# Attention and two MLPs in one kernel: loads issued in another order, and one addition of the weights' decoding moved from VectorE to GpSimd

## The chip, the cores and the metric

The kernel runs on one core of a Trainium2 chip. The metric is the device time of one execution in microseconds (us). TensorE multiplies matrices, VectorE and ScalarE work on elements, GpSimd does small element work and issues some of the transfers, and SP's queue issues most of the others.

## The reference

Three stages follow one another on 2 x 3008 rows of 256 columns. All is float32.

```python
scores = (1.0 / S) * z @ z.T                 # per batch, z is 3008 x 64
x = u * (np.maximum(scores, 0.0) ** 2 @ v)   # attention without a softmax
h = x @ moe_w_in                             # 6016 x 256 @ 256 x 2048
P = a[0] + a[1]*h + a[2]*h**2 + a[3]*h**3
Q = 1.0 + abs(b[0])*abs(h) + abs(b[1])*h**2
x = (P / (Q + 1e-06)) @ moe_w_out            # 2048 x 256
h = x @ moe2_w_in
out = (np.maximum(h, 0) + alpha * np.minimum(h, 0)) @ moe2_w_out
```

The four weight matrices arrive as 64-bit floats, each as a low and a high 32-bit word.

## The kernel before

Every float32 operand of TensorE is split into a high part that the fast format holds and the rest, a low part; a product is the sum of three matmuls. For z the two parts are stacked in one tile (zA), with a swapped copy (zB).

Attention (stream A) takes 12 blocks of 512 query columns (6 for each batch). A block has 12 steps, kp = 0 to 11, of 256 key rows each: `a_scores` makes the scores, ScalarE and VectorE make relu, square and the parts ahi and alo, and `a_values`, three steps behind (LAG_A), multiplies them with the parts of v (vt). At the end of a block `a_end` multiplies with u (the tile ut, loaded by `a_u`) and stores the result in DRAM (xd). The first MLP (m1) works on 12 blocks of 512 rows, each in 8 steps of 256 hidden columns, and stores to DRAM (x2d); the second MLP (m2) does the same and stores the output.

The main program emits steps. For the first 36 it emits stream A alone; then it weaves 40 steps of m1 into the rest of stream A; then the rest of m1 with m2. Beside that it decodes weights: `load_w` (16 tiles of m1's weights, in the first 36 steps and shortly after) and `spill_w` (16 tiles of m2's, every fifth step but not in steps 64 to 75, where batch 1's v is loaded). `decode` is a chain of six VectorE instructions and one ScalarE instruction on 128x512 words (L148 to L158); the last adds the part from the low word. The raw words come through GpSimd's queue into two buffers (tag "wr").

A scheduler orders each engine's instructions by its own idea of time and by a priority, which is the place in the program (`tc.high_priority(EARLY)` moves some forward). The order on each engine and queue is fixed when the kernel runs: an instruction that waits holds all behind it. A tile waits until a buffer of its tag is free. The raw v of batch 1, the raw z of batch 1, ut, x and the results share two buffers (tag "raw", RAW = 2); for batch 0, raw z and v have many early buffers (tag "big").

Of the kernel before, what the change touches and what calls it, by code (L numbers as in the profile page):

```python
# [7 lines left out]
F32 = mybir.dt.float32  # L8
# [4 lines left out]
ALU = mybir.AluOpType  # L13
# [28 lines left out]
def relu2_attention_rational_mlp_prelu_mlp(  # L42
# [47 lines left out]
    def raw_tile(nm, early=False):  # L90

        if early:
            return big.tile([P, 1024], F32, tag="big", name=nm)
        return tmp.tile([P, 1024], F32, tag="raw", name=nm, bufs=RAW)
# [16 lines left out]
    def load_rows(t, src, r0, n):  # L111

        full, rest = divmod(n, P)
        if full:
            nc.sync.dma_start(
                out=t[:, 0:full, :],
                in_=src[r0 : r0 + full * P, :].rearrange("(c p) d -> p c d", p=P),
            )
        if rest:
            for p0 in (0, HALF):  # L120
                nc.sync.dma_start(
                    out=t[p0 : p0 + rest, full, :], in_=src[r0 + full * P : r0 + n, :]
                )

    vt = {}

    def load_v(b, kp):

        raw = raw_tile("vraw", b == 0)
        r3 = raw.rearrange("p (c d) -> p c d", c=4)  # L130
        r0 = kp * 2 * P
        load_rows(r3, v[b], r0, min(S - r0, 4 * P))
        for i in range(2):
            t = big.tile([P, 2, 2, D], F32R, tag="big", name="vt")
            split(t[:, 0], t[:, 1], r3[:, 2 * i : 2 * i + 2, :], on_act=b > 0 or (kp > 0 and i == 0))
            if kp + i == NKP - 1:

                h2 = t[HALF:P, 0, 1].bitcast(F32)
                nc.vector.tensor_tensor(t[HALF:P, 1, 1], h2, h2, ALU.subtract)
            vt[b, kp + i] = t  # L140

    def decode(raw):

        low, high = raw[:, :, 0], raw[:, :, 1]
        w = tmp.tile([P, 2, 512], F32R, tag="t", name="dec", bufs=TT)
        val, ulp = w[:, 0].bitcast(F32), w[:, 1].bitcast(F32)

        nc.vector.tensor_scalar(val, high.bitcast(F32), BOUND, -BOUND, ALU.min, ALU.max)  # L148
        nc.scalar.activation(val, val, AF.Copy, scale=2.0**-112)
        vali = val.bitcast(I32)  # L150
        nc.vector.tensor_scalar(
            vali, vali, 3, 2**31 - 1, ALU.logical_shift_left, ALU.bitwise_and
        )
        nc.vector.scalar_tensor_tensor(vali, high, -(2**31), vali, ALU.bitwise_and, ALU.bitwise_or)

        nc.vector.tensor_scalar(ulp.bitcast(I32), vali, -(2**23), None, ALU.bitwise_and)
        nc.vector.scalar_tensor_tensor(ulp, low.bitcast(U32), 2.0**-52, ulp, ALU.mult, ALU.mult)
        nc.vector.tensor_tensor(val, val, ulp, ALU.add)  # L158
        return w

    def words(src):
# [71 lines left out]
    def load_z(b, g):  # L233

        raw = raw_tile("zraw", b == 0)
        n = qn[g]
        nc.sync.dma_start(out=raw[:, 0:n], in_=zt[b, :, g * QB : g * QB + n])
        if n % P:
            nc.sync.dma_start(out=raw[:, n : n + HALF], in_=zt[b, :, S - HALF : S])
            n += HALF  # L240
        t = zp.tile([P, QB], F32R, tag="z", name="zA")
        with tc.high_priority(EARLY):
            nc.vector.tensor_copy(t[:, 0:n], raw[:, 0:n])
            nc.vector.tensor_tensor(
                t[HALF:P, 0:n], raw[HALF:P, 0:n], t[HALF:P, 0:n].bitcast(F32), ALU.subtract
            )
        if (b, g) == (0, 0):
            zB[b, g] = zp.tile([P, QB], F32R, tag="z", name="zB")
            nc.scalar.copy(zB[b, g][HALF:P, 0:n], raw[HALF:P, 0:n])
            nc.vector.tensor_tensor(  # L250
                zB[b, g][0:HALF, 0:n], raw[0:HALF, 0:n], t[0:HALF, 0:n].bitcast(F32), ALU.subtract
            )
        zA[b, g] = t
# [16 lines left out]
    def a_begin(b, j):  # L270

        if (b, j) in zB:
            return
        n = qn[j]
        t = zp.tile([P, QB], F32R, tag="z", name="zB")
        for p0 in (0, HALF):
            nc.sync.dma_start(
                out=t[p0 : p0 + HALF, :n].bitcast(F32),
                in_=zA[b, j][HALF - p0 : P - p0, :n].bitcast(F32),
            )  # L280
        zB[b, j] = t
# [110 lines left out]
    def a_u(b, j):  # L392
        n = qn[j]
        t = tmp.tile([P, ND, QB], F32, tag="raw", name="ut", bufs=RAW)
        nc.sync.dma_start(
            out=t[:, :, :n],
            in_=ut_in[b, :, j * QB : j * QB + n].rearrange("(e p) s -> p e s", p=P),
        )
        uts[b, j] = t
# [7 lines left out]
        nc.sync.dma_start(out=xd[b, j][:, :, :n], in_=t[:, :, :n])  # L407


    def load_x(src, n, pool):  # L410
        raw = tmp.tile([P, ND, QB], F32, tag="raw", name="xr", bufs=RAW)
        nc.sync.dma_start(out=raw[:, :, :n], in_=src[:, :, :n])
        return split_x(raw, n, pool)

    def split_x(src, n, pool):
        hs, ls = [], []
        for d in range(ND):
            hi = pool.tile([P, QB], F32R, tag="x", name="xhi")
            lo = pool.tile([P, QB], F32R, tag="x", name="xlo")
            split(hi[:, :n], lo[:, :n], src[:, d, :n])  # L420
            hs.append(hi)
            ls.append(lo)
        return hs, ls
# [83 lines left out]
    g2 = {}  # L507
    acc2 = {}

    def m2_begin(q):  # L510
        if q != LAST:
            x2[q] = load_x(x2d[q], bn[q], late["x"])

    def m2_hidden(q, jp):
        n = bn[q]
# [15 lines left out]
    def m2_last(q, jp):  # L531

        n, r0 = bn[q], q * QB
        if jp == 0:
            acc2[q] = [
                psa.tile([P, ND, QB], F32, tag=f"acc{e}", name="acce")[:, 0] for e in range(ND)
            ]
        hi, lo = g2.pop((q, jp))
        for e in range(ND):
            acc = acc2[q][e][:, :n]  # L540
            half(acc, e, w2ot[jp], hi, lo, n, jp == 0, jp == NJ - 1)
            if jp < NJ - 1:
                continue

            parts = [(0, n)] if e == 0 else [(0, n // 2), (n // 2, n)]
            for i, (c0, c1) in enumerate(parts):
                t = tmp.tile([P, 2 * QB], F32, tag="t", name="oe", bufs=TT)
                copy, queue = ((nc.scalar.copy, nc.sync), (nc.vector.tensor_copy, nc.scalar))[i]
                copy(t[:, 0 : c1 - c0], acc[:, c0:c1])
                queue.dma_start(  # L550
                    out=out[e * P : (e + 1) * P, r0 + c0 : r0 + c1], in_=t[:, 0 : c1 - c0]
                )

    def m2_back(q, jp):
        if q == LAST:
# [21 lines left out]
    def a_stream():  # L577

        pend = []

        def drain(upto):
            while len(pend) > upto:
                q, kp = pend.pop(0)
                a_values(*q, kp)
                if kp == NKP - 2:
                    a_u(*q)
                if kp == NKP - 1:
                    a_end(*q)

        for q in blocks:  # L590
            b, j = q
            if q == (0, 0):
                load_z(0, 0)
                load_z(0, 1)
                load_v(0, 0)
            a_begin(b, j)
            for kp in range(NKP):
                if q == (0, 0) and kp % 2 == 0:
                    if kp + 4 < NKP:
                        load_z(0, kp // 2 + 2)  # L600
                    if kp + 2 < NKP:
                        load_v(0, kp + 2)
                a_scores(b, j, kp)
                pend.append((q, kp))
                drain(LAG_A)
                if j == NQ - 1 and b + 1 < B:
                    if kp % 2 == 1:
                        load_z(b + 1, kp // 2)
                    if (kp - LAG_A) % 2 == 1 and kp > LAG_A:
                        load_v(b + 1, kp - LAG_A - 1)  # L610
                if j == 0 and b > 0:
                    k0 = kp + NKP - LAG_A - 1
                    if k0 < NKP and k0 % 2 == 0:
                        load_v(b, k0)
                yield
        drain(0)
        yield
# [21 lines left out]

    ga = a_stream()  # L640
    g1s = m_stream(m1_hidden, m1_back, m1_begin, m1_end, range(NB), LAG_M, x1)
    g2s = m_stream(m2_hidden, m2_back, m2_begin, m2_end, range(NB), LAG_M)
    w1 = [w for jp in range(NJ) for w in ((w1i, w1it, jp, True), (w1o, w1ot, jp, False))]
    w2 = [w for jp in range(NJ) for w in ((w2i, w2it, jp, True), (w2o, w2ot, jp, False))]
    fills = list(w2)
# [18 lines left out]
    for st in range(HEAD, na):  # L664
# [11 lines left out]
        if st >= na - 1 - NKP + LAG_A and fills:  # L676
            for _ in range(2):
                if len(fills) > 4 - (BIG - 28):
                    f = fills.pop(0)
                    fill_w(f[1], f[2])  # L680

    zctx.close()
    assert len(fills) <= BIG - 2 * NJ - NKP + 4
    late["x"] = ctx.enter_context(tc.tile_pool(name="xp2", bufs=XP))
    late["w"] = ctx.enter_context(tc.tile_pool(name="late", bufs=max(len(fills), 1)))
    for f in fills:
        fill_w(f[1], f[2])

    left = (NB - 1) * NJ - KEEP
    steps = NB * NJ - n1  # L690
    for st in range(steps):
# [45 lines left out]
```

## Time and profile before

| | us |
|---|---|
| median of 3 runs | 1559.61 |
| lowest and highest | 1559.13 and 1562.73 |
| the profiled execution | 1560.04 |
| its span, first to last instruction | 1558.3 |

The granted TensorE clock was 1.00 over the span. In the page an engine's line gives its busy time, its share of the span and its number of instructions. In the order of time a row gives start, duration, engine, line, operation and tiles, and in brackets how long the engine had been idle and what ended that. "SPq" is SP's queue.

### The profile page before, as it was taken

The numbers are of one execution on the slowest core, as the hardware profiler recorded it, in microseconds if no ns is written. First come the engines' busy times: TensorE is split into PE (matmuls) and PEld (weight loads), VectorE is DVE, ScalarE is ACT, GpSimd is POOL, SyncE is SP. The second block draws the span as 40 slices with busy tenths as digits, with TensorE's granted clock in tenths as the row PEclk, the third lists the DMA queues.
The fourth block names the chain that finished last, engine by engine and source line by source line (L and its number), as shares of the span: only waits on it lengthen the run. The fifth ranks groups of instructions, "written<-read, shape, count | busy, mean of one in ns | idle before, by whom it ended". The sixth has DMA issues, their size and how long they took to land.

```text
span 1558.3 us, 18042 instructions
## 1 busy us (share of the span) xinstructions
PE 1547.0 (99%) x6896; PEld 1284.4 (82%) x6896; DVE 1397.4 (90%) x1495; ACT 1194.3 (77%) x1465; POOL 53.9 (3%) x93
## 2 busy tenths in 40 slices
PE   9999999999999999999999999999999999999998
PEld 7888888888887888888788888888888888888888
DVE  8999999999899999898999989999899999898864
ACT  8999998998999989897667666666666666666654
POOL 1010000000000000001000000000000000000000
PEclk9999999999999999999999999999999999999999
DMA  6342111331212212135101000000101010001000
GB/s 190 115 129 87 54 55 41 115 119 34 82 34 68 74 55 68 53 95 178 38 1 41 26 29 14 28 27 28 41 0 41 1 41 28 24 0 42 14 1 24
DMA packets 37910, 83.16 MB, mean 53 GB/s; under 512 B 5168, under 2 KB 15040, under 8 KB 37824
## 3 DMA queue, kind: packets, MB, share of 16 engines
q1 hardware_dynamic: 26128, 48.34, 9.6%
q0 software_dynamic: 11552, 33.57, 6.9%
q8 instruction: 54, 0.88, 0.2%
q14 instruction: 32, 0.26, 0.1%
q10 hardware_dynamic: 144, 0.10, 0.0%
HBM read 52.70 MB, written 26.48 MB: 51 GB/s over the span
## 4 chain that ended last, share of the span: by engine, by line
PE 84%; DVE 6%; issue 4%; DMA 2%; ACT 2%; POOL 0%; SPq 0%; POOLq 0%; DVEq 0%; ACTq 0%
PE acc L363 20%; PE acca L363 11%; PE h L343 10%; PE h L344 10%; PE h L345 10%; PE acc L372 10%; PE acca L372 5%; PE s L322 3%; PE s L323 3%; DMA zraw<-in_z_dram 1%; PE acce L353 1%; DVE alo L109 1%; DVE ghi L484 0%; ACT r L328 0%; DMA wraw<-in_moe_w_out_dram 0%
## 5 line engine op out<-in xcount | busy, mean ns | idle before, releaser
L363 PE MATMUL acc<-ghi,w 128*128 128x512 f32 (+1 forms) x1472 | 366.5, 387 | 0.0
L363 PEld LDWEIGHTS acc<-ghi,w 128*128 128x128 f32 x1472 | 275.3, 188 | 54.7 <-ACT ghi L106 0.3
L343 PE MATMUL h<-xhi,w 128*128 128x512 f32 (+1 forms) x768 | 295.4, 386 | 1.2 <-DVE t L477 0.8
L344 PE MATMUL h<-xlo,w 128*128 128x512 f32 (+1 forms) x768 | 295.9, 386 | 0.0
L345 PE MATMUL h<-xhi,w 128*128 128x512 f32 (+1 forms) x768 | 295.8, 385 | 0.0
L363 PE MATMUL acca<-ahi,vt 128*128 128x512 f32 (+1 forms) x1152 | 289.4, 386 | 2.4 <-ACT ahi L106 1.9
L363 PEld LDWEIGHTS acca<-ahi,vt 128*128 128x128 f32 x1152 | 215.5, 188 | 46.1 <-ACT ahi L106 4.0
L522 ACT ACTIVATE m<-h,sal 128x512 f32<-128x512 f32 (+1 forms) x192 | 127.3, 680 | 111.4 <-PE h L345 109.9
L470 ACT ACTIVATE sq<-h 128x1024 f32<-128x1024 f32 (+1 forms) x96 | 96.9, 1010 | 139.7 <-PE h L345 130.1
L372 PE MATMUL acc<-glo,w 128*128 128x512 f32 (+1 forms) x736 | 195.9, 387 | 0.3 <-DVE glo L487 0.3
L109 DVE TENSOR_TENSOR alo<-r,ahi 128x1024 fp32r<-128x1024 f32 (+2 forms) x133 | 158.2, 1190 | 30.3 <-ACT ahi L106 11.0
L343 PEld LDWEIGHTS h<-xhi,w 128*128 128x128 f32 x768 | 144.1, 188 | 31.7 <-ACT sq L480 1.2
L344 PEld LDWEIGHTS h<-xlo,w 128*128 128x128 f32 x768 | 144.2, 188 | 28.7 <-DVE xlo L109 1.1
L345 PEld LDWEIGHTS h<-xhi,w 128*128 128x128 f32 x768 | 144.2, 188 | 27.5
L109 DVE TENSOR_TENSOR glo<-m,ghi 128x1024 fp32r<-128x1024 f32 (+1 forms) x96 | 115.1, 1199 | 55.5 <-PE acc L363 42.3
L372 PEld LDWEIGHTS acc<-glo,w 128*128 128x128 f32 x736 | 137.7, 188 | 28.2 <-DVE glo L487 0.8
L523 DVE SCALAR_TENSOR_TENSOR m<-h,sg,m 128x512 f32<-128x512 f32 (+1 forms) x192 | 138.1, 735 | 16.7 <-ACT m L522 15.3
L328 ACT ACTIVATE r<-r 128x1024 f32<-128x1024 f32 (+1 forms) x143 | 150.0, 1051 | 2.0
L372 PE MATMUL acca<-alo,vt 128*128 128x512 f32 (+1 forms) x552 | 149.3, 386 | 0.2 <-DVE alo L109 0.2
L325 ACT ACTIVATE r<-s 128x512 f32<-128x512 f32 (+1 forms) x244 | 135.3, 589 | 17.3 <-DVE t L486 13.8
L106 ACT CAST ahi<-r 128x1024 fp32r<-128x1024 f32 (+2 forms) x133 | 135.9, 1024 | 1.3 <-PE acc L372 0.8
L474 DVE SCALAR_TENSOR_TENSOR ab<-sq,cb,ab 128x1024 f32<-128x1024 f32 (+1 forms) x96 | 120.7, 1257 | 11.4 <-ACT ab L471 11.3
(92 smaller groups left out, 2135.3 us busy)
## 6 DMA issues: line engine op xcount, KB each, us to landing
wraw<-in_moe_w_in_dram POOLq DMA_DIRECT2D x16, 512.0 KB, 4.2
wraw<-in_moe_w_out_dram POOLq DMA_DIRECT2D x16, 512.0 KB, 3.9
wd<-dec POOLq DMA_DIRECT2D x32, 256.0 KB, 2.3
w<-wd POOLq DMA_DIRECT2D x16, 512.0 KB, 3.9
x2d<-x SPq DMA_DIRECT2D x11, 512.0 KB, 2.6
xr<-x2d SPq DMA_DIRECT2D x11, 512.0 KB, 3.3
out_dram<-ot SPq DMA_DIRECT2D x11, 512.0 KB, 2.9
vraw<-in_v_dram SPq DMA_DIRECT2D x10, 512.0 KB, 5.6
```

The lines of the kernel that those rows point to most:

```text
L106: nc.scalar.copy(dst_hi, src)
L109: nc.vector.tensor_tensor(dst_lo, src, dst_hi.bitcast(F32), ALU.subtract)
L325: nc.scalar.activation(r[:, i, :n], s, AF.Relu, scale=1.0 / S)
L328: nc.scalar.activation(r[:, :, :n], r[:, :, :n], AF.Square)
L343: nc.tensor.matmul(acc, w_hi, hi, start=first, stop=False)
L344: nc.tensor.matmul(acc, w_hi, lo, start=False, stop=False)
L345: nc.tensor.matmul(acc, w_lo, hi, start=False, stop=last)
L363: nc.tensor.matmul(acc[:, e, :n], w[:, k, i, e * P : (e + 1) * P], hi[i], start=first and i == 0 and k == 0, stop=False,)
L372: nc.tensor.matmul(acc[:, e, :n], w[:, 0, i, e * P : (e + 1) * P], lo[i], start=False, stop=last and i == both - 1,)
L474: nc.vector.scalar_tensor_tensor(ab, sq, b1, ab, ALU.mult, ALU.add)
L522: nc.scalar.activation(t[:, i], h, AF.Copy, scale=sal[:, f : f + 1])
L523: nc.vector.scalar_tensor_tensor(t[:, i], h, sg[:, f : f + 1], t[:, i], ALU.mult, ALU.max)
```

## The change

Six things change. (1) In the first block, groups 3 and 4 of z are loaded at step 2 and group 5 at step 4 (before: 3 at step 2, 4 at step 4, 5 at step 6). (2) The first two ut tiles get a one-column GpSimd copy that reads the last z tile, so their loads wait for it. (3) The loads of v and their splits are two functions; for batch 1 the raw words go into the two buffers of the weight words, and each load is issued one group of two steps before its split. (4) The addition at the end of `decode` runs on GpSimd. (5) `load_x` returns the raw tile; m2's first load is emitted before the attention's buffers are given up and its split before the last loop. (6) The last block's second half is copied by ScalarE and stored in one piece, as the first half is.

```diff
-        raw = raw_tile("vraw", b == 0)
+        if b == 0:
+            raw = raw_tile("vraw", True)
+        else:
+            raw = wr.tile([P, 1024], F32, tag="wr", name="vraw")
...
+        vraw[b, kp] = r3
+
+    def split_v(b, kp):
+        r3 = vraw.pop((b, kp))
...
-        nc.vector.tensor_tensor(val, val, ulp, ALU.add)
+        nc.gpsimd.tensor_tensor(val, val, ulp, ALU.add)
...
+        if b == 0 and j < RAW:
+
+            nc.gpsimd.tensor_copy(t[:, 0, 0:1], zA[0, NQ - 1][:, 0:1].bitcast(F32))
...
-        return split_x(raw, n, pool)
+        return raw
...
+    def m2_load(q):
+        x2r[q] = load_x(x2d[q], bn[q])
+
     def m2_begin(q):
-        if q != LAST:
-            x2[q] = load_x(x2d[q], bn[q], late["x"])
+        if q == LAST:
+            return
+        if q not in x2r:
+            m2_load(q)
+        x2[q] = split_x(x2r.pop(q), bn[q], late["x"])
...
-            parts = [(0, n)] if e == 0 else [(0, n // 2), (n // 2, n)]
-            for i, (c0, c1) in enumerate(parts):
-                t = tmp.tile([P, 2 * QB], F32, tag="t", name="oe", bufs=TT)
-                copy, queue = ((nc.scalar.copy, nc.sync), (nc.vector.tensor_copy, nc.scalar))[i]
...
+            nc.scalar.copy(t[:, 0:n], acc)
+            nc.sync.dma_start(out=out[e * P : (e + 1) * P, r0 : r0 + n], in_=t[:, 0:n])
...
-                    if kp + 4 < NKP:
-                        load_z(0, kp // 2 + 2)
+                    for g in {0: (2,), 2: (3, 4), 4: (5,)}.get(kp, ()):
+                        load_z(0, g)
...
-                    if (kp - LAG_A) % 2 == 1 and kp > LAG_A:
-                        load_v(b + 1, kp - LAG_A - 1)
-                if j == 0 and b > 0:
-                    k0 = kp + NKP - LAG_A - 1
-                    if k0 < NKP and k0 % 2 == 0:
-                        load_v(b, k0)
+
+                k0 = kp - LAG_A - 1 if j == NQ - 1 else kp + NKP - LAG_A - 1
+                b1 = b + (j == NQ - 1)
+                if (j == NQ - 1 or j == 0) and 0 < b1 < B and k0 % 2 == 0:
+                    if 0 <= k0 < NKP:
+                        split_v(b1, k0)
+                    if 0 <= k0 + 2 < NKP:
+                        load_v(b1, k0 + 2)
...
+    m2_load(0)
     zctx.close()
...
+    m2_begin(0)
```

## Rows read from the trace of the kernel before

**Rows 1.** The page, busy us and share of the span.
```profile
PE 1547.0 (99%) x6896; PEld 1284.4 (82%) x6896; DVE 1397.4 (90%) x1495; ACT 1194.3 (77%) x1465; POOL 53.9 (3%) x93
```

**Rows 2.** TensorE's waits, ten rows: us in total, times, longest.
```profile
PE acca L363 <- ACT ahi L106: 1.9, 3, 1.5
PE wps L101 <- DVE one L211: 1.4, 1, 1.4
PE sp L322 <- DVE zA L244: 0.9, 1, 0.9
PE h L343 <- DVE t L477: 0.8, 1, 0.8
...
PE acca L363 <- DVE ahi L337: 0.2, 1, 0.2
```

**Rows 3.** The chain that ended last, in order of time: start, us, what.
```profile
3.17 8.22 DMA zraw<-in_z_dram
...
158.38 1.81 PE acca L363 x8
```

**Rows 4.** Order of time, 0 to 14 us, SP's queue and TensorE.
```profile
2.10 1.02 SPq L395 DMA_DIRECT2D ut<-in_u_dram  x2
...
8.69 0.39 PE L323 MATMUL s<-zB,zA 128*128 128x512 f32 x1
...
13.31 0.47 PE L322 MATMUL sp<-zA 128*128 128x512 f32 x1
```

**Rows 5.** Order of time, 10 to 38 us, around the last z group.
```profile
10.89 0.43 SPq L239 DMA_DIRECT2D zraw<-in_z_dram  x1
...
36.28 0.69 DVE L244 TENSOR_TENSOR zA<-zraw,zA 64x512 fp32r<-64x512 f32 x1
...
37.12 0.47 PE L322 MATMUL sp<-zA 128*128 128x512 f32 x1 [0.88 <-DVE zA L244]
```

**Rows 6.** Order of time, 320 to 328 us, around a v load.
```profile
320.48 0.38 SPq L115 DMA_DIRECT2D vraw<-in_v_dram  x1
...
325.33 0.62 ACT L106 CAST vt<-vraw 128x512 fp32r<-128x512 f32 x1 [2.88 <-DMA vraw<-in_v_dram]
...
327.76 1.89 PE L363 MATMUL acca<-ahi,vt 128*128 128x448 f32 x8 [1.48 <-ACT ahi L106]
```

**Rows 7.** Order of time, SP's queue at 736 us.
```profile
736.78 0.54 SPq L412 DMA_DIRECT2D xr<-x2d  x1
```

**Rows 8.** Tile wraw: ns min/median/max; who waited for it (us, times).
```profile
L165 POOL COPY wraw<-zA x2: 653/948/1242, 17.2 to 18.4; 128x1 f32<-128x1 f32 x2
...
DVE dec L148: 2.8, 3
```

**Rows 9.** Tile dec: ns min/median/max, first and last start.
```profile
L158 DVE TENSOR_TENSOR dec<-dec x32: 679/684/693, 30.8 to 664.7; 128x512 f32<-128x512 f32 x32
...
L108 DVE CAST w<-dec x16: 406/422/487, 31.5 to 136.3; 128x512 fp32r<-128x512 f32 x16
```

**Rows 10.** Groups of GpSimd: busy us, mean ns, idle before.
```profile
L221 POOL TENSOR_TENSOR sal<-sc,sg 128x16 f32<-128x16 f32 x1 | 0.2, 215 | 0.0
...
L224 POOL TENSOR_TENSOR cb<-sc,cb 128x2 f32<-128x2 f32 x1 | 0.2, 187 | 0.0
```

**Rows 11.** Order of time, VectorE and TensorE, 17 to 61 us.
```profile
17.18 1.23 DVE L109 TENSOR_TENSOR alo<-r,ahi 128x1024 fp32r<-128x1024 f32 x1
...
57.97 1.22 DVE L109 TENSOR_TENSOR alo<-r,ahi 128x1024 fp32r<-128x1024 f32 x1
...
60.40 1.07 PE L372 MATMUL acca<-alo,vt 128*128 128x512 f32 x4
```

**Rows 12.** Busy us by stretch: PE, PEld, DVE, ACT, POOL, clock, DMA.
```profile
40.00:140.00 100.00, 100.00 (x443) 82.66 (x442) 95.16 (x156) 92.51 (x115) 10.84 (x15) 1.00 0.38 118
```

**Rows 13.** Tile oe, the last store: ns min/median/max.
```profile
L549 ACT COPY oe<-acce x2: 319/400/480, 1553.0 to 1554.1; 128x384 f32<-128x384 f32 x1, 128x192 f32<-128x192 f32 x1
...
L549 DVE COPY oe<-acce x1: 358/358/358, 1554.4 to 1554.4; 128x192 f32<-128x192 f32 x1
```

More of the change, by code (lines that the diff above doesn't have):

```diff
@@ L125, in relu2_attention_rational_mlp_prelu_mlp @@
     vt = {}
+    vraw = {}
     def load_v(b, kp):
-        raw = raw_tile("vraw", b == 0)
+        if b == 0:
+            raw = raw_tile("vraw", True)
+        else:
+            raw = wr.tile([P, 1024], F32, tag="wr", name="vraw")
         r3 = raw.rearrange("p (c d) -> p c d", c=4)
@@ L407, in a_end, with load_x @@
         nc.sync.dma_start(out=xd[b, j][:, :, :n], in_=t[:, :, :n])
-    def load_x(src, n, pool):
+    def load_x(src, n):
         raw = tmp.tile([P, ND, QB], F32, tag="raw", name="xr", bufs=RAW)
         nc.sync.dma_start(out=raw[:, :, :n], in_=src[:, :, :n])
-        return split_x(raw, n, pool)
+        return raw
     def split_x(src, n, pool):
@@ L508, in relu2_attention_rational_mlp_prelu_mlp @@
     acc2 = {}
+    x2r = {}
+    def m2_load(q):
+        x2r[q] = load_x(x2d[q], bn[q])
     def m2_begin(q):
-        if q != LAST:
-            x2[q] = load_x(x2d[q], bn[q], late["x"])
+        if q == LAST:
[3 more added lines that the diff above has]
+        x2[q] = split_x(x2r.pop(q), bn[q], late["x"])
     def m2_hidden(q, jp):
@@ L543, in m2_last @@
                 continue
-            parts = [(0, n)] if e == 0 else [(0, n // 2), (n // 2, n)]
-            for i, (c0, c1) in enumerate(parts):
-                t = tmp.tile([P, 2 * QB], F32, tag="t", name="oe", bufs=TT)
-                copy, queue = ((nc.scalar.copy, nc.sync), (nc.vector.tensor_copy, nc.scalar))[i]
[L549 to L552, printed above, removed]
+            t = tmp.tile([P, 2 * QB], F32, tag="t", name="oe", bufs=TT)
+            nc.scalar.copy(t[:, 0:n], acc)
+            nc.sync.dma_start(out=out[e * P : (e + 1) * P, r0 : r0 + n], in_=t[:, 0:n])
     def m2_back(q, jp):
@@ L595, in a_stream @@
                 load_v(0, 0)
+                split_v(0, 0)
             a_begin(b, j)
@@ L598, in a_stream @@
                 if q == (0, 0) and kp % 2 == 0:
-                    if kp + 4 < NKP:
-                        load_z(0, kp // 2 + 2)
+                    for g in {0: (2,), 2: (3, 4), 4: (5,)}.get(kp, ()):
+                        load_z(0, g)
                     if kp + 2 < NKP:
                         load_v(0, kp + 2)
+                        split_v(0, kp + 2)
                 a_scores(b, j, kp)
@@ L641, in relu2_attention_rational_mlp_prelu_mlp @@
     g1s = m_stream(m1_hidden, m1_back, m1_begin, m1_end, range(NB), LAG_M, x1)
-    g2s = m_stream(m2_hidden, m2_back, m2_begin, m2_end, range(NB), LAG_M)
+    g2s = m_stream(m2_hidden, m2_back, m2_begin, m2_end, range(NB), LAG_M, x2)
     w1 = [w for jp in range(NJ) for w in ((w1i, w1it, jp, True), (w1o, w1ot, jp, False))]
```

## The prediction

> **What bounds the kernel now.** I began with the page's busy times [rows 1]: TensorE is busy for 1547.0 us of a span of 1558.3, VectorE for 90% of it. So only what TensorE loses can be won back. The second view is the list of TensorE's own waits [rows 2]: ten rows, 6.6 us in all, of which 1.4 us lies before the first data and no single one is over 1.5 us. The third is the chain of work in order of time [rows 3], which gives the pace: eight full matmuls in 1.81 us, 0.227 us each. With it the order of time shows losses that the list of waits leaves out: the distance between two starts, less the matmuls between. Four places of some size lie where the edits touch.
>
> (a) The start. Between the starts at 8.69 and 13.31 us lie 13 matmuls, 13 x 0.227 = 2.95 us of 4.62, so 1.7 us are lost [rows 4]. The matmul at 13.31 needs the third group of z, whose transfer is on the chain from 3.17 on for 8.2 us [rows 3]. Ahead of it in SP's queue stand two ut loads at 2.10 [rows 4].
> (b) At 36 us. TensorE's start at 37.12 follows 0.9 us of waiting for VectorE's L244 on the last z group; with the restart about 1.0. The raw words of that group had been issued at 10.89, while L244 ran at 36.28 [rows 5]. So VectorE's order is late here, not the transfer.
> (c) At 327 us. A v load is issued only at 320.48; ScalarE stands still in its order for 2.9 us until it has landed, starts the cast at 325.33, and then makes ahi late for the values at 327.76: 1.5 us, about 1.6 with the restart [rows 6].
> (d) The passage from attention to the two MLPs: 0.8 us of waiting for L477 [rows 2], about 0.9 with the restart.
>
> These are 1.7 + 1.0 + 1.6 + 0.9 = 5.2 us. The rest of the list is 6.6 - 1.4 - 1.9 - 0.9 - 0.8 = 1.6 us in small pieces.
>
> **The change, part by part.**
>
> Start: each of the first two ut loads gets a GpSimd copy in front that waits for the last z group, so they leave the first 10 us. The third z group then has 1 MB less before it. The loss need not vanish, since the values matmuls in the same stretch wait for ScalarE [rows 2]. Bounds 0 and -1.7; I take half, -0.8. The two added copies stand in GpSimd's queue, with weight loads behind them; like the copies already there they cost 0.65 to 1.24 us each [rows 8]. A weight load that they make late is the same kind of delay as the one that the additions cause, and is priced with it.
>
> z order: groups 3 and 4 come with one step, the last at step 4 in place of 6. As its L243 and L244 now stand earlier in the program, I expect them earlier in VectorE's order. Bounds 0 and -1.0; I take -1.0, since L244 has to come only 1 us sooner and its raw words were asked for 25 us before.
>
> v loads of batch 1: they leave the two raw buffers, which they shared with z, ut, x and the results, for the two buffers of the weight words, and each is issued one group ahead of its split. During these steps no weights are spilled. A group is two attention steps with at least 32 matmuls (some 7 us), against 4.8 us from the issue at 320.48 to the cast [rows 6]. On SP's queue a v load that waits for its buffer would hold the z loads, the zB copies and the xd stores behind it; that can come only from the last spill before, or from a split that is late. Bounds 0 and -1.6; I take all, -1.6.
>
> m2's first load and split come earlier in the program. The load hardly can: it takes one of two raw buffers and goes out at 736.78, directly behind the last xd store [rows 7]. What can move is the order of the splits behind it, while the wait at L477 is the first MLP's own chain. Bounds 0 and -0.9; I take -0.2.
>
> Last store: two copies, ScalarE's 0.32 us and then VectorE's 0.36, become one of 384 columns, which took 0.48 for the other half [rows 13]: 0.2 us less, and a transfer of twice the size behind it. I take 0.
>
> The additions: 32 instructions of 0.684 us leave VectorE [rows 9], 22 us in all. TensorE gains nothing from that by itself, as it waits for VectorE only in the places above. What they cost on GpSimd is not in the trace. The nearest rows are its two-input instructions of 2 and 16 columns, 187 and 215 ns [rows 10]: 2 ns a column, so 0.19 + 512 x 0.002 = 1.2 us, an estimate from these two rows; VectorE's 0.684 is the lower bound. What matters more is whether VectorE can work beside it. The trace shows that GpSimd waits: a copy of a single column took up to 1.24 us [rows 8] while VectorE ran a subtraction of 1.23 us from 17.18 [rows 11]. The other direction isn't shown. The Trainium skill (SBUF — State Buffer, Who interferes with whom) says that a VectorE instruction with two SBUF inputs contends with a GpSimd instruction that reads SBUF, and that the one that comes second is blocked until the first has finished. By that rule each addition would stop VectorE for its own length; by VectorE's freed time alone there would be no loss.
>
> I work out both from rows. Of the 16 decodes before 140 us, 15 fall between 40 and 140 [rows 9], where VectorE is busy 95.2 of 100 us [rows 12]. If each addition holds VectorE for 1.2 us in place of its own 0.684, that is 15 x 0.52 = 7.8 us more: 103.0 us of work in 100. The 3.0 us too many meet a lead: an alo that ends at 59.19 is used at 60.40 [rows 11], 1.2 us ahead, the closest that I found in this stretch; most are near 3 us ahead. So it costs TensorE 0 to 3 us. In addition, the next weight load may now stand behind the addition on GpSimd's queue, 1.2 us late; three decodes wait for their load already, 2.8 us in all [rows 8], and there VectorE stops in its order, with alo behind. If that hits half of the 15, it is 7 x 1.2 = 8.4 us more, of which VectorE's 4.8 us of idle time can take some: up to 8 us in all for TensorE once the lead is used up. Without any exclusion the cost is 0. I take +1.0, nearer to the free end, since the lead and the idle time come first; bounds 0 and +8. The other 16 additions are spread up to 665 us [rows 9], one in 33 us, against VectorE's 10% of idle time: 0.
>
> Sum: -0.8 - 1.0 - 1.6 - 0.2 + 1.0 = -2.6 us. The profiled execution took 1560.04 us, its span 1558.3 and 1.7 around it, so it comes to 1557.4; the median of the runs shown is 1559.61, 0.4 lower, and gives **1557.0 us**.
>
> **Rivals.**
> *VectorE becomes the bound while the weights are decoded (slower).* The place is 40 to 140 us. It decides from the point where an addition costs VectorE more than its idle time and a lead of 3 us can carry: (4.8 + 3)/15 = 0.52 us above 0.684, so from 1.2 us of blocking on, exactly my estimate. For it: 95% busy, and the copies that were blocked. Against it: the lead, and that part of VectorE's work may run beside. With the late loads +8, and -2 from the moves: 1565.6. The Trainium skill's rule above speaks for it. Chance 0.16.
> *All places pay and the additions are free (faster).* -5.2 us give 1554.4, with the small waits -6.8 and 1552.8. For it: the edits touch all four places. Against it: (a) is shared with ScalarE and (d) has another cause. Chance 0.31.
> *The stalls only move.* The order on every engine is drawn anew; other waits of 0.5 to 1.5 us take the place of those removed, as ten such are left now in an order that was no worse. About 1559.5. Chance 0.19.
> *My forecast*, 1555 to 1558.5: 0.34.
>
> **Numbers.** 0.3% of 1559.6 is 4.7 us, about what a measurement tells from no change: below 1554.9 is faster, above 1564.3 slower. The forecast and the third rival lie between: same 0.53; faster 0.31; slower 0.16. The range reaches down to all places and all small waits, 1552.8, and up to no gain with some half of the worst additions, 1559.6 + 4.4 = 1564.0.
>
> **What would show it.** Right: no TensorE wait near 36 and 327 us, v loads of batch 1 issued 5 us or more before their casts, ut loads after 35 us, L158 on GpSimd near 1.2 us. For the slower rival: TensorE waits for alo or ahi between 40 and 140 us, VectorE instructions beside L158 that last longer than before or gaps of 1 us there, weight loads that land after their decode is due. The prediction is wrong if the time moves by over 5 us, and right by luck if a GpSimd loss of several us cancels a gain.

## The result, and the profile after

The changed kernel takes 1583.41 us, median of four runs (1580.56 to 1584.01), beside 1559.86 for the kernel before: a ratio of 1.0143, 95% interval 1.0131 to 1.0155. It is 23.5 us slower. The forecast was 1557.0 with a range of 1552.8 to 1564.0. The profiled execution took 1583.44 us, with a span of 1581.7.

The page's busy times of the kernel after answer to [rows 1]:

```profile
PE 1556.1 (98%) x6896; PEld 1285.9 (81%) x6896; DVE 1389.1 (88%) x1462; ACT 1194.8 (76%) x1465; POOL 111.5 (7%) x127
```

VectorE has fewer instructions and is busy 8.3 us less, GpSimd 57.6 us more. By busy time alone nothing became a bound. TensorE's own waits (in total, times, longest), the answer to [rows 2]:

```profile
PE s L331 <- ACT r L334: 13.4, 15, 2.4
PE sp L331 <- ACT r L336: 2.5, 3, 1.6
PE wps L101 <- DVE one L220: 1.4, 1, 1.4
PE h L352 <- DVE t L489: 1.1, 1, 1.1
```

The waits at 36 and 327 us are gone, as the moves were to bring. In their place stand 18 waits, 15.9 us in all, for ScalarE's relu of the scores (L334, L336), which frees the score tile that TensorE writes next. In the kernel before, such waits came to one:

```profile
PE s L322 <- ACT r L325: 0.4, 1, 0.4
```

The waits are not all that was lost: TensorE's busy time also grew, by 9.1 us. Of that 3.4 us are two falls of its clock (last section); the rest isn't taken apart.

What holds ScalarE is in the list of waits of all engines, first one line of the kernel before, then four of the kernel after:

```profile
ACT dec L149 <- DVE dec L148: 12.4, 11, 5.2
```

```profile
ACT dec L158 <- DVE dec L157: 21.5, 14, 5.1
...
DVE w L108 <- POOL dec L167: 12.6, 11, 1.5
...
ACT dec L199 <- POOL dec L167: 11.0, 8, 2.6
DVE dec L108 <- POOL dec L167: 10.0, 8, 1.5
```

ScalarE's wait in the middle of a decode (L158 now, L149 before) grew by 9.1 us. The sum of the weights' parts (L167 now, L158 before) is waited for 27 times, 33.6 us in all, by the instruction that reads it; before, VectorE made the sum itself. The tile view of dec (ns min/median/max, first and last start) shows how long the addition takes, and that VectorE's instructions grow beside it (the addition on VectorE had a spread of 14 ns, [rows 9]):

```profile
L160 DVE TENSOR_SCALAR dec<-dec x32: 412/421/1406, 25.5 to 680.1; 128x512 int32<-128x512 int32 x32
L163 DVE SCALAR_TENSOR_TENSOR dec<-wraw,dec x32: 680/687/1669, 26.0 to 681.7; 128x512 int32<-128x512 int32 x32
...
L167 POOL TENSOR_TENSOR dec<-dec x32: 1278/1908/3881, 29.3 to 685.9; 128x512 f32<-128x512 f32 x32
```

The shortest addition, 1.28 us, is near the estimate of 1.2. The median is 1.9 and the longest 3.9. The two stages differ: of the 16 additions before 150 us twelve took 1.28 to 1.50 us, of the 16 after that thirteen took 2.1 us or more. Two stretches of the order of time show a long one of each stage. The first is a decode of the load stage:

```profile
97.82 0.69 DVE L166 SCALAR_TENSOR_TENSOR dec<-wraw,dec 128x512 f32<-128x512 uint32 x1
...
98.43 1.22 DVE L109 TENSOR_TENSOR alo<-r,ahi 128x1024 fp32r<-128x1024 f32 x1
98.70 2.10 POOL L167 TENSOR_TENSOR dec<-dec 128x512 f32<-128x512 f32 x1 [4.25 <-DVE dec L166]
...
100.83 0.43 DVE L108 CAST w<-dec 128x512 fp32r<-128x512 f32 x1 [1.18 <-POOL dec L167]
101.18 0.52 DVE L157 TENSOR_SCALAR dec<-wraw 128x512 f32<-128x512 f32 x1
...
101.72 0.63 ACT L158 ACTIVATE dec<-dec 128x512 f32<-128x512 f32 x1 [2.32 <-DVE dec L157]
...
103.20 1.07 ACT L334 ACTIVATE r<-s 128x512 f32<-128x512 f32 x2
...
103.84 0.50 PE L331 MATMUL s<-zA 128*128 128x512 f32 x1 [1.18 <-ACT r L334]
```

Read it from the bottom. TensorE waits 1.18 us for a relu; the relu stands on ScalarE behind a cast and L158 of the next decode, before which ScalarE was idle for 2.32 us; that waits for VectorE's L157, which stands behind the cast L108; and the cast waits for the addition. The addition began 0.27 us after alo. Alo ends at 98.43 + 1.22 = 99.65, the addition at 100.80, 1.15 us later: about the length that it has when nothing runs beside it. By these times it got next to nothing done while alo ran.

The second is a spill decode, with the longest addition:

```profile
256.46 1.22 DVE L499 TENSOR_TENSOR glo<-t,sq 128x1024 fp32r<-128x1024 f32 x1
256.69 3.88 POOL L167 TENSOR_TENSOR dec<-dec 128x512 f32<-128x512 f32 x1 [26.09 <-DVE dec L166]
...
257.60 0.69 DVE L109 TENSOR_TENSOR xlo<-xr,xhi 128x512 fp32r<-128x512 f32 x1
258.20 1.22 DVE L109 TENSOR_TENSOR alo<-r,ahi 128x1024 fp32r<-128x1024 f32 x1
260.60 0.91 ACT L199 ACTIVATE dec<-dec,sg 128x256 fp32r<-128x256 f32 x2 [2.60 <-POOL dec L167]
...
264.45 0.58 ACT L334 ACTIVATE r<-s 128x512 f32<-128x512 f32 x1
...
265.09 0.50 PE L331 MATMUL s<-zA 128*128 128x512 f32 x1 [2.39 <-ACT r L334]
```

Three VectorE instructions with two inputs follow one another without a pause until 258.20 + 1.22 = 259.42; the addition, begun at 256.69, ends 1.15 us after that again. ScalarE, in its order, stands 2.60 us for it, the relu slips, and TensorE loses 2.39 us.

Busy times by stretch, the kernel after (columns as in [rows 12]):

```profile
40.00:140.00 100.00, 95.15 (x408) 75.08 (x407) 87.32 (x132) 84.15 (x105) 28.79 (x27) 1.00 0.36 108
...
410.00:680.00 270.00, 264.91 (x1144) 213.13 (x1143) 236.18 (x242) 236.02 (x296) 33.32 (x35) 0.99 0.20 63
```

From 40 to 140 us TensorE does 408 matmuls in place of 443, and VectorE is less busy than before. VectorE waits; it has not run out of time.

### The profile page after: what moved, and what is told of

It is laid out like the page before. It is cut to its first block, busy times and chain, and to the rows that moved or that the text cites. A ratio compares the mean times of both kernels' runs of the same rounds, so it can differ in the third digit from the quotient of the medians.

```text
span 1581.7 us, 18066 instructions
## 1 busy us (share of the span) xinstructions
PE 1556.1 (98%) x6896; PEld 1285.9 (81%) x6896; DVE 1389.1 (88%) x1462; ACT 1194.8 (76%) x1465; POOL 111.5 (7%) x127
## 4 chain that ended last, share of the span: by engine, by line
PE 59%; DVE 5%; ACT 5%; issue 1%; POOL 1%; DMA 0%; SPq 0%; POOLq 0%; DVEq 0%; ACTq 0%
PE acc L372 17%; PE h L353 9%; PE h L352 9%; PE h L354 9%; PE acc L381 9%; PE acca L372 2%; PE acca L381 1%; POOL dec L167 1%; PE acce L362 1%; PE s L331 1%; ACT r L334 1%; ACT ahi L106 1%; PE s L332 1%; ACT t L484 1%; ACT ab L483 1%
## 5 line engine op out<-in xcount | busy, mean ns | idle before, releaser
L109 DVE TENSOR_TENSOR alo<-r,ahi 128x1024 fp32r<-128x1024 f32 (+2 forms) x133 | 162.9, 1226 | 33.2 <-PE acc L372 13.3
L334 ACT ACTIVATE r<-s 128x512 f32<-128x512 f32 (+1 forms) x244 | 134.9, 590 | 21.4 <-DVE t L498 20.2
```

Source lines behind the costliest of these rows:

```text
L109: nc.vector.tensor_tensor(dst_lo, src, dst_hi.bitcast(F32), ALU.subtract)
L334: nc.scalar.activation(r[:, i, :n], s, AF.Relu, scale=1.0 / S)
```

## The experiments

**The moves and the addition, each alone.** First all moves with the addition back on VectorE:

```diff
-        nc.gpsimd.tensor_tensor(val, val, ulp, ALU.add)
+        nc.vector.tensor_tensor(val, val, ulp, ALU.add)
```

> The changed kernel with the addition back on VectorE, so only the moved loads are left. If the addition on GpSimd is the whole loss, by waiting or by blocking, this is at 1553 to 1559 us, below the kernel before by what the moves win (0 to 6 us), and the TensorE waits at 36 and 327 us are gone. If the moved loads lose the time (a third theory), it is at 1575 us or more.

Measured: 1557.82 us beside 1560.73, ratio 0.9982 (0.9973 to 0.9992). The moves win 2.9 us, and this version takes less time than both kernels. Below it is called the moves alone. Then the kernel before with only the addition on GpSimd:

> The kernel before with only the addition on GpSimd, no load moved. If the addition is the whole loss: 1580 to 1588 us, as the changed kernel has it or a little more, since the moves' gain is missing. If the moved loads lose the time: within 3 us of 1560. If it is only the two together, in between.

Measured: 1590.76, ratio 1.0191 (1.0174 to 1.0208), +30.6 us. So the addition is the whole loss: 30.6 without the moves, 1583.4 - 1557.8 = 25.6 with them. The kernel before was timed anew beside each group of runs and came to 1559.9 to 1560.7, so differences between groups are known to about 1 us.

**Which additions.** On GpSimd only in the 16 decodes of the load stage, then only in the 16 spill decodes (decode takes the engine as an argument):

```diff
-    def decode(raw):
+    def decode(raw, add):
...
-        nc.gpsimd.tensor_tensor(val, val, ulp, ALU.add)
+        add.tensor_tensor(val, val, ulp, ALU.add)
```

> Moved loads, and GpSimd adds only in the 16 decodes of the first MLP's weights, before 145 us; VectorE adds in the other 16. In the changed kernel the stretch from 57 to 143 us became 8 us longer. Both theories, waiting in order and blocking, expect the moves-only time plus 6 to 10 us, lost before 150 us. If the additions of the second MLP's weights carry the loss instead, it is within 2 us of moves only.

> Moved loads, and GpSimd adds only in the 16 decodes of the second MLP's weights, from 150 us on; TensorE's order is that of the changed kernel, instruction by instruction. In the changed kernel the stretches from 143 to 272 and from 337 to 697 us became some 17 us longer with 16 such decodes. Waiting in order expects moves only plus 12 to 18 us: one addition in 30 us that stops ScalarE and VectorE for 1 to 3 us. Blocking alone expects little here, moves only plus 0 to 4 us, as VectorE had 8% idle time in these stretches.

Measured: 1566.09 (ratio 1.0036, 1.0023 to 1.0049), 8.3 us above the moves alone, with the same order of instructions on TensorE as these. And 1572.44 (1.0075, 1.0060 to 1.0090), 14.6 us above, with the same order on TensorE as the changed kernel. 8.3 + 14.6 = 22.9 of the 25.6. The larger part lies where the forecast had put nothing. In the first, VectorE waits for the sums just as it does in the changed kernel's load stage, 12.6 us in 11 places (L108 for L167).

**The load stage: what in a GpSimd instruction costs.** All additions on VectorE, and beside each of the first 16 decodes an instruction of GpSimd whose result nobody reads. An addition:

```diff
+        if not opened:
+            two = ulp.rearrange("p (n t) -> p n t", t=2)
+            nc.gpsimd.tensor_tensor(raw[:, 0:256, :].bitcast(F32), two, two, ALU.add)
```

> Moved loads, all additions on VectorE; beside each of the first 16 decodes GpSimd adds the low word's part to itself, 128x512, into the raw words' buffer, started by the same VectorE instruction and ahead of the same weight load in its queue, and nobody waits for its result but that buffer. Work of the same size and place is added, which the output doesn't use. If VectorE loses by being blocked (and by late weight loads), this is moves only plus 8 us or more, since VectorE keeps its own additions too. If the loss comes from engines that wait in order for GpSimd's result, it is moves only plus 0 to 4 us.

A write of zeros in its place:

```diff
+        if not opened:
+            nc.gpsimd.memset(raw.bitcast(F32), 0.0)
```

> All additions on VectorE, the moves kept; beside each of the first 16 decodes GpSimd writes zeros over the raw words that have been read (no input from SBUF, nobody reads what it writes). The unread addition in the same place cost 10.7 us over the moves alone (1568.5 against 1557.8). If an instruction of GpSimd that reads SBUF is what holds VectorE: 1558 to 1560, and VectorE's instructions beside the writes keep their lengths (420 and 687 ns). If it is GpSimd's queue that costs, the weight load standing behind a 1 to 2 us instruction: 1565 to 1569, with VectorE's instructions at their usual lengths. If any GpSimd work on SBUF blocks VectorE: 1565 to 1569 with VectorE's instructions lengthened by about 1 us.

And a copy, with one input:

```diff
+        if not opened:
+            nc.gpsimd.tensor_copy(raw[:, 0:256, :].bitcast(F32), ulp.rearrange("p (n t) -> p n t", t=2))
```

> All additions on VectorE, the moves kept; beside each of the first 16 decodes GpSimd copies 512 columns of the low parts into the raw words that have been read (one SBUF input), and nobody reads the copy. Two SBUF inputs gave +10.7 us over the moves alone (1568.5), none +2.3 (1560.15). If any SBUF input makes GpSimd hold VectorE: 1564 to 1569, with VectorE's instructions beside the copies longer by 0.5 us or more. If only two inputs do: 1559 to 1561, with VectorE's instructions at their usual lengths.

The three have the same order of instructions on TensorE, VectorE, ScalarE and SyncE, so they compare directly:

| GpSimd instruction | SBUF inputs | its median us | median of the runs, us | ratio to before (95%) |
|---|---|---|---|---|
| zeros | 0 | 0.95 | 1560.15 | 0.9999 (0.9989 to 1.0008) |
| copy | 1 | 1.34 | 1564.96 | 1.0030 (1.0019 to 1.0040) |
| addition | 2 | 1.74 | 1568.51 | 1.0050 (1.0036 to 1.0065) |

The tile views, first of wraw and then of dec (ns min/median/max), of the writes of zeros:

```profile
L169 POOL MEMSET wraw<- x16: 947/952/1167, 28.8 to 137.1; 128x1024 f32 x16
```

```profile
L167 DVE TENSOR_TENSOR dec<-dec x32: 673/684/693, 28.8 to 664.2; 128x512 f32<-128x512 f32 x32
```

of the copies:

```profile
L169 POOL COPY wraw<-dec x16: 741/1338/4357, 28.6 to 141.7; 128x512 f32<-128x512 f32 x16
```

```profile
L167 DVE TENSOR_TENSOR dec<-dec x32: 678/691/1102, 28.6 to 668.8; 128x512 f32<-128x512 f32 x32
```

and of the unread additions:

```profile
L170 POOL TENSOR_TENSOR wraw<-dec x16: 1142/1742/4757, 29.3 to 146.7; 128x512 f32<-128x512 f32 x16
```

```profile
L167 DVE TENSOR_TENSOR dec<-dec x32: 683/691/1531, 29.3 to 673.3; 128x512 f32<-128x512 f32 x32
```

Beside the zeros VectorE's own addition takes 0.69 us at most, and the longest write 1.17; beside a GpSimd instruction that reads SBUF it takes up to 1.10 and 1.53, and that instruction up to 4.4 and 4.8. Length alone doesn't explain it, as the shortest copy, 0.74 us, is shorter than any of the writes. Nobody reads a result in any of the three, so 4.8 us for the first input and 3.6 for the second (5.0 and 2.9 when each is taken from its own timing of the kernel before) lie in the two engines getting in each other's way, in the weight load that stands longer behind GpSimd's instruction, and in what follows from both. To the last belongs TensorE's clock: with the copies and with the additions it fell once in this stage in the profiled execution, 1.7 us each, and not with the zeros (last section). The zeros bound what the place in the queue costs by itself: 1560.15 - 1557.82 = 2.3 us, an order of its own included.

These runs show what the hold alone can do, not its share in the real additions. With the real ones in this stage VectorE mostly stands and waits for the sum, 12.6 us, and its instructions run over their usual lengths by 5.3 us in all (eight of them); with the unread ones nothing is waited for, and that overrun is 12.5 us (sixteen). The two ways aren't separated further here.

The question of the queue was also put to the changed kernel, with the weight words loaded by SyncE:

```diff
-        nc.gpsimd.dma_start(out=raw, in_=src.rearrange("(c p) f -> p c f", p=P))
+        nc.sync.dma_start(out=raw, in_=src.rearrange("(c p) f -> p c f", p=P))
```

> The changed kernel with the loads of the raw weight words issued by SyncE, so that none stands behind an addition on GpSimd. If late weight loads carry a good part of the loss: 1574 to 1579 and a load stage (first to third xd store) of some 87 us in place of 93.3. If the blocking carries it: within 2 us of 1583.4, load stage 92 to 94 us. It can be slower by SyncE's own order, as its stores wait for ScalarE.

Measured: 1581.73 (1.0137, 1.0122 to 1.0152), 1.7 us less than the changed kernel, with the order on TensorE unchanged. The two intervals overlap, so the difference is not clear of the noise. Late weight loads are a small part at most.

**The spill decodes: hold or wait.** First all readers of the sum later: the load decode's split one decode later, the rest of a spill two steps later (its tile is held as long):

```diff
-        v3 = raw_w(src, jp, wide)[:, 0].bitcast(F32).rearrange("p (c d) -> p c d", c=2)
+        w = raw_w(src, jp, wide)
+        held_w()
+        held.append((w, store, jp))
...
+        if st % SP == 2 and late_s:
+            spill_rest()
```

> All 32 additions on GpSimd as in the changed kernel, but the instructions that read a sum come later: a load's split one decode later, a spill's two attention steps later. If waiting in order for the sum is the loss, most of the 24 us against before is won back: moves only plus 0 to 6 us, and the waits of VectorE and ScalarE for the addition (38.8 us in the changed kernel) fall under 5 us. If blocking is the loss, it stays at 1578 us or more.

Measured: 1577.21 (1.0105, 1.0088 to 1.0122), 6.2 us less than the changed kernel. It is no clean test: VectorE still waits for the addition 14 times, and ScalarE's relu now waits 5.3 us for stores out of the tiles that are held longer. Then an unread addition in the spill decodes (its operands lie two words apart), all real ones on VectorE:

```diff
+        if opened:
+            hi = high.bitcast(F32)
+            nc.gpsimd.tensor_tensor(low.bitcast(F32), hi, hi, ALU.add)
```

> All additions on VectorE, the moves kept; beside each of the 16 spill decodes GpSimd does an addition of the same size into raw words that have been read, and nobody reads its result. With the real additions in these 16 decodes the loss over the moves was 14.6 us (1572.4 against 1557.8). If ScalarE and VectorE waiting in order for the result is the cause there: 1558 to 1561, stages of 130 and 338 us (third to fifth and sixth to eleventh xd store) as with the moves alone. If the blocking is the cause: 1567 to 1572, stages of 134 to 136 and 343 to 346 us. Between the two each holds its share.

Measured: 1565.18 (1.0033, 1.0021 to 1.0045), 7.4 us above the moves alone. VectorE's instructions grow (its own addition up to 1.53 us), but TensorE's wait for relu is only 1.4 us in place of 10.8 with the real additions, and 2.7 us are one wait at 292 us, 12 us behind the nearest addition. That pointed at the order of the instructions, which is drawn anew for every kernel. The next was to show the wait alone, with zeros written twice and one column of them copied by the engine that reads the sum:

> The counterpart of the unread additions in the spill decodes, which gave +7.4 us over the moves alone: the wait without the hold. All additions on VectorE, the moves kept; in each of the 16 spill decodes GpSimd writes zeros twice over the raw words that have been read (some 1.9 us, no SBUF input), and ScalarE in the narrow spills, VectorE in the wide ones, reads one column of that before it goes on, so it stands in order as long as it stood for the addition. If waiting in order carries the other half of the 14.6 us: 1563 to 1566, with TensorE again waiting for ScalarE's r by some 6 to 10 us. If the hold carries all and the unread additions only found easier places: 1558 to 1560.

Measured: 1563.04 (1.0017, 1.0008 to 1.0027). It doesn't show what it was made for: the copies stand later in their engines' order, and neither has any idle time before it. So the last three put the dependence into the real reader (its scale is read from what GpSimd wrote) and add a control:

```diff
+        if opened:
+            for _ in range(2):
+                nc.gpsimd.memset(raw[:, 0:480, :].bitcast(F32), 1.0)
+            done.append(raw[:, 0, 0:1].bitcast(F32))
...
+        seen = done.pop()
...
+            nc.vector.tensor_scalar(w[:, 1], w[:, 0].bitcast(F32), seen, None, ALU.mult)
...
-                nc.scalar.activation(hi, lo.bitcast(F32), AF.Copy, scale=f)
+                nc.scalar.activation(hi, lo.bitcast(F32), AF.Copy, scale=seen)
```

> All additions on VectorE, the moves kept; in each of the 16 spill decodes GpSimd writes ones twice over the raw words that have been read (1.8 us, no SBUF input), and the first reader of the sum (ScalarE's scaling, or VectorE's cast in the wide spills) takes its factor from there, so that it cannot start before. The narrow spills are scaled by one in place of the column's sign. If waiting in order is the larger part of the 14.6 us: 1566 to 1572 and TensorE waits for ScalarE's r by 6 us or more. If the hold on VectorE is: 1558 to 1561.

The second has the spill decode's unread addition and a write of one column in place of the two writes, the third the write of one column alone:

> As the kernel that waits without a hold, but what is waited for is an unread addition of 512 columns (2.6 us where it ran before) and a write of one column behind it; the order on TensorE is the same but for 4 matmuls. Hold and wait together should give the loss of the real additions in these decodes: 1570 to 1574, with VectorE instructions longer by up to 1 us. If the hold adds nothing to a wait: within 2 us of the kernel that only waits.

> The same two readers, but GpSimd writes only the one column that they read (some 0.1 to 0.2 us), so there is next to nothing to wait for. What is left is an order drawn anew. If the order has no price: 1557 to 1559, as the moves alone. If the order alone costs what the unread additions lost at 292 us: about 1560 to 1561.

Measured: control 1563.18 (1.0020, 1.0011 to 1.0029), writes 1564.13 (1.0022, 1.0013 to 1.0032), addition 1576.99 (1.0104, 1.0088 to 1.0119). None lies in a range that had been expected of it. The control alone is 5.4 us above the moves, though there is next to nothing to wait for. Its order is another one, and a wait at 290 us (1.8 us) is again in it; that the rest is the order too is likely but not shown. The writes of 1.8 us, in an order of their own, come 1.0 above the control, less than either kernel's runs spread. The addition comes 13.8 us above the control, and these two have the same order of instructions on TensorE, VectorE and ScalarE and the same order of SyncE's transfers: nothing in this difference is an order drawn anew. TensorE's wait for relu, of the control, of the writes, and of the addition; the fourth line is ScalarE's wait for the write behind the addition (VectorE waits 2.2 us more), and with the writes no engine waits for them:

```profile
PE s L337 <- ACT r L340: 3.0, 4, 0.8
```

```profile
PE s L338 <- ACT r L341: 2.6, 4, 0.8
```

```profile
PE s L339 <- ACT r L342: 12.3, 15, 3.2
...
ACT dec L206 <- POOL wraw L171: 10.0, 8, 2.1
```

The same decode in the last two, in order of time, first with the writes:

```profile
491.41 1.87 POOL L170 MEMSET wraw<- 128x960 f32 x2 [10.57 <-DVE dec L166]
493.72 0.90 ACT L205 ACTIVATE dec<-dec,wraw 128x256 fp32r<-128x256 f32 x2
```

then with the addition:

```profile
497.01 4.29 POOL L170 TENSOR_TENSOR wraw<-wraw 128x512 f32<-128x512 f32 x1 [10.93 <-DVE dec L166]
...
501.49 0.91 ACT L206 ACTIVATE dec<-dec,wraw 128x256 fp32r<-128x256 f32 x2 [2.10 <-POOL wraw L171]
...
506.89 0.80 PE L339 MATMUL s<-zA 128*128 128x512 f32 x1 [3.20 <-ACT r L342]
```

The writes are done 0.44 us before ScalarE's turn. The addition is dragged out to 4.29 us, ScalarE stands 2.10, and TensorE loses 3.20. So in these kernels wait and hold aren't two causes side by side: there is a wait because the addition, dragged out beside VectorE's two-input work, comes later than its reader's place. A write as long as the dragged addition was not run; it might make the reader wait as well.

**Half the columns.**

```diff
-        nc.gpsimd.tensor_tensor(val, val, ulp, ALU.add)
+        nc.gpsimd.tensor_tensor(val[:, 0:256], val[:, 0:256], ulp[:, 0:256], ALU.add)
+        nc.vector.tensor_tensor(val[:, 256:512], val[:, 256:512], ulp[:, 256:512], ALU.add)
```

> The changed kernel with each addition cut in two: GpSimd adds 256 of the 512 columns, VectorE the other 256. If the loss goes with the time for which GpSimd holds VectorE, half of the 25.6 us: about 1570. If it goes with the number of GpSimd additions and waits, whatever their length: 1578 to 1583. If VectorE's half and GpSimd's half simply ran side by side, the decode would be shorter than on VectorE alone: 1556 to 1558.

Measured: 1570.03 (1.0065, 1.0050 to 1.0080), 12.2 us above the moves alone: half of 25.6. The 256-column addition takes 1.32 us on average, the one of 512 columns 1.82.

## Why the prediction was wrong, step by step

**The moves: right.** Forecast -3.6 in all, measured -2.9. Busy times by stretch, the kernel before and then the moves alone:

```profile
0.00:40.00 40.00, 37.05 (x149) 28.47 (x150) 32.40 (x54) 33.84 (x45) 7.15 (x16) 1.00 0.60 185
...
280.00:340.00 60.00, 58.17 (x269) 49.83 (x269) 55.31 (x60) 54.97 (x75) 1.70 (x3) 1.00 0.36 108
```

```profile
0.00:40.00 40.00, 38.22 (x157) 30.36 (x158) 35.27 (x59) 35.61 (x47) 8.35 (x19) 1.00 0.66 207
...
280.00:340.00 60.00, 59.85 (x278) 51.54 (x278) 57.49 (x62) 57.57 (x79) 1.99 (x3) 1.00 0.43 130
```

Start and z order: forecast -1.8, TensorE is busy 1.2 us more by 40 us. The ut loads leave the first 10 us, but go out at 22.7 us in the kernel after, not after 35. v loads: forecast -1.6, won 1.7; in the kernel after the second one of batch 1 is issued at 293.83 and first cast at 306.04, 12 us later. m2's begin: forecast -0.2. "The load hardly can" was wrong: with the moves alone the first one goes out at 672.89, not at 736.78. It brought nothing, as the wait behind it [rows 2] grew from 0.8 to 1.4 us.

**The additions before 140 us: VectorE's stops sized about right, what absorbs them wrong.** The forecast took +1.0, "since the lead and the idle time come first", with bounds of 0 and +8. Measured: +8.3. The kernel with these additions alone took 1566.09, near the 1565.6 of the slower rival.

How much VectorE stops was nearly right. It waits 12.6 us for sums and its instructions run over by 5.3 us; less the 16 x 0.684 = 10.9 us that left it, this is 7.0 us, where the forecast had 7.8. What kept TensorE from paying was wrong: the forecast let the idle time and the lead of alo take most of it, and TensorE lost 8.3 us, no less than these stops. The lead didn't cover it, because the loss went by another way: cast, L157, ScalarE's L158, the relu behind it, and then scores in place of values. In the kernel with these additions alone TensorE waits 3.9 us for relu between 40 and 140 us and 1.1 us for alo and ahi.

That the upper bound of 8 was met is in part luck. It was made of 0 to 3 us for the hold and the rest for late weight loads, and these cost some 2 us at most (the loads by SyncE, the zeros). That VectorE would wait for the sum itself, in its own order, had no term.

The Trainium skill (SBUF — State Buffer, Who interferes with whom) says that a VectorE instruction with two SBUF inputs contends with a GpSimd instruction that reads SBUF and not with one that only writes it. For the addition of two inputs the runs agree: up to 1.53 us for 0.69 beside unread additions, 0.69 at most beside writes of zeros. The rule was named in the prediction, and nearly all of its effect was then written off.

**The additions after 140 us: the step that failed.** "One in 33 us, against VectorE's 10% of idle time: 0." Measured: +14.6. An engine's mean idle share was no cover for an instruction in the middle of a chain. The idle time is where VectorE itself waits; most additions meet it in the middle of two-input work and take 2.1 to 3.9 us in place of 0.68, VectorE and ScalarE wait 21 us for the sums, and ScalarE's reader is in order with the relu on which the next scores depend. Up to some 5 us of the 14.6 may be the order drawn anew, since the control lost 5.4 in one of its own; how much it is in the changed kernel's order isn't separated. That such a loss needs no new order is shown: with the order of all three engines fixed, an addition in front of the reader cost 13.8 us.

**GpSimd's duration.** The estimate of 1.2 us was right for an addition that runs alone (1.28), as most of the first 16 do. The mean of all is 1.82, and the rest follows from what VectorE does beside it.

**What would show it.** Of the slower rival's signs, longer VectorE instructions came. TensorE's waits for alo or ahi between 40 and 140 us came once in the changed kernel, 0.5 us at 97 us; the longer ones, 4.1 us, were for relu. Late weight loads were no large part.

## What to carry to other kernels

In this kernel work that was taken from VectorE to GpSimd, and that reads SBUF, was not taken off VectorE. Price such a move as serial with VectorE's two-input instructions, at its length alone plus what is ahead of it; add the wait of the next instruction that reads the result, and look for who stands in order behind that reader. Idle share covers only what nobody waits for soon: follow the chain from the moved instruction's reader to TensorE before writing a zero. A change that mixes moves with an engine swap is run in two halves first: here the moves alone were the faster kernel, at 1557.8.

## What the runs showed of the hardware that was not expected

An addition on GpSimd made no visible progress while VectorE ran two-input instructions back to back: it began at 256.69, two of the three began after it, and it ended 1.15 us after the last of them. The Trainium skill (SBUF — State Buffer, Summary: rules for kernel authors) says that of a VectorE instruction with two SBUF inputs and a GpSimd instruction that reads SBUF the second to issue is blocked until the first finishes. The trace agrees that one blocks the other, but here the one already waiting was passed over twice by VectorE. The other direction is shown too: in the kernel after, VectorE's L163 took up to 1.67 us for 0.69.

One SBUF input on GpSimd is enough. Beside copies VectorE's addition took up to 1.10 us, and the kernel was 4.8 us slower than with writes of zeros in the same order.

A write on GpSimd and a longer VectorE instruction of a single input were also seen together. In the kernel with zeros, in order of time:

```profile
98.51 0.72 POOL L177 DMA_DIRECT2D wraw<-in_moe_w_out_dram  x1 [0.30 <-POOL wraw L169]
98.85 0.60 DVE L160 TENSOR_SCALAR dec<-dec 128x512 int32<-128x512 int32 x1
...
131.07 0.95 POOL L169 MEMSET wraw<- 128x1024 f32 x1 [3.56 <-DVE dec L166]
131.12 1.18 DVE L157 TENSOR_SCALAR dec<-wraw 128x512 f32<-128x512 f32 x1
```

L157 and L160 take 0.42 us elsewhere. L157 ended 0.28 us behind the zeros that began just before it, and beside the issue of a weight load on GpSimd these two took about 0.60, seven times in that kernel. The Trainium skill (SBUF — State Buffer, Who interferes with whom) says that VectorE in its modes with two ports contends with GpSimd, whichever issues first, and counts tensor_scalar among the instructions that can enter them; these rows agree with it, but no run here took them apart.

TensorE's clock fell behind some of the waits, so that they cost more than their length. In the kernel after, the granted clock was 0.50, the lower of its two levels (1.2 GHz), from 266.6 to 270.0 us, behind the wait of 2.39 us at 265.09, and for as long from 515.8 on, behind one of 1.85 us. Matmuls then started 0.42 us apart in place of 0.23, which loses 1.7 us each time. With the moves alone the clock stayed at the upper level (1.00) in every stretch up to 680 us. A wait of 2.54 us at 291 us, in the kernel with two writes in the spill decodes, was followed by no such fall.
